# An FFT and MLP-mixer kernel: five PSUM banks for the first chunk, token products ahead of a relu, and a later start of a fold

## The chip, the cores and the metric

The kernel runs on one core of a Trainium2 chip. A core has TensorE (PE: matrix products, which go to PSUM), VectorE (DVE), ScalarE (ACT), GpSimd (POOL) and a sync engine (SP) that issues DMAs; GpSimd and ScalarE issue DMAs too. Each engine works through its own list of instructions in order, and semaphores hold an instruction until what it needs is done. The metric is the device time of one execution in microseconds (us): the median of three runs before was 605.32 us (605.01 to 606.32).

## The reference

The input x is 8 batches of 3008 rows by 256 features. The real part of a Fourier transform over both dimensions goes into a mixer of two layers, one over rows (tokens) and one over features (channels):

```python
X = np.fft.fft(np.fft.fft(x, axis=1), axis=2)
x = X.real                                    # 8 x 3008 x 256
h = np.maximum(x.transpose(0, 2, 1) @ w_tok1, 0.0) @ w_tok2   # 3008 -> 256 -> 3008
u = x + h.transpose(0, 2, 1)
h2 = np.maximum(u @ w_ch1, 0.0) @ w_ch2       # 256 -> 1536 -> 256
out = u + h2
```

## The kernel before

The 3008 rows are taken as 47 x 64, so that the transform over rows is two short transforms, and symmetries of the real part halve the work. For each batch there is a *front*, which makes the u of that batch, and a *main loop*, which makes the channel layer from it.

**The front.** `fold(b, eng)` (L321) adds mirrored parts of the loaded input tiles `xp` and `xm`: four groups of additions (`fa`, `fb`, and three `eo`), then a last step for one row; 17 steps in all. For batches 0 and 1 VectorE does it, for later ones GpSimd. `xm` comes from an indirect gather that GpSimd issues (L109). `front(b)` (L414) then makes `z` (`pz` products, L424), `w` (`pw`, L450 and L452), `rot` (`prot`, L459), the transform `yt` of three chunks (`y(c)`: `py`, L476), the first token layer `uu` (`tok1`: `pt`, L526, with a relu per half `th`), and the second token layer (`tok2(c)`: `pu`, L497), whose sum with `yt` is `ut`, the u of chunk c. A chunk is 512 rows (64 x 8); there are six.

For batch 0 the products `carried()` (`ph`, L403 and L405) must be done as well: they carry w_tok1 through the row transform into `hp` and `hq`, which `tok1` of all batches reads.

**The main loop.** For each chunk there are 12 slots, one for each 128 of the 1536 hidden channels; slot = 12 x chunk + ct. `mm1` (L586) does two products of 128x512 (`pc`, L593, for the halves h of the 256 features) and a relu into the tile `c1`, by ScalarE (`act`, L97) or, for the ct in `on_v`, by VectorE (`ts`, L84). In batch 0 the first three slots are done in one call: the three products for h=0 first, then the three for h=1. The second layer of a chunk is interleaved with the slots of the next: `mm2` (`po`, L698) at every third slot for the first two chunks of batch 0, and later `mm2_seven`, a product of seven multiplications instead of eight (`pa`, `pb`, L643). The first `po` products are at slot 14, and they need all twelve relus of chunk 0. `weight_sums` (L576) makes the weight tiles for `mm2_seven` (`t1w` to `t4w`) on GpSimd, once, at slot 1.

**The order of the work.** It is written out by hand (`manual_schedule`). The functions above are generators, and `take(g, n)` runs n steps of one. L725 to L755 are the prologue, which brings batch 0 to the end of `tok2(0)`. In the loop, `own_at` tells at which slots a step of batch 0's own front is taken: the remaining step of `y(1)`, `tok2(1)`, `y(2)`, and so on, so that the u of chunk 2 is made at slots 20 and 22. Steps of the next batch's front (`nxt`) follow from slot 20 on, the first being `pz`. `fold1`, the fold of batch 1, is taken from slot 9: one step at odd slots, two at even ones. GpSimd's `load_x(2)` at slot 21 fills the `xp` and `xm` that this fold reads.

**PSUM.** There are eight banks, in three kinds: `ps_mm` (tag mm, three, used in turn: `ph`, `pc`), `ps_f` (tag f, three: `pz`, `pw`, `py`, `pt`, `pu`), and `ps_out` (o0 and o1, one each: `po`, `pa`, `pb`). A product that starts in a bank waits until the one that was there has been read.

Of the kernel before, what the change touches and what calls it, by code (L numbers as in the profile page):

```python
# [36 lines left out]
def kernel(  # L37
# [9 lines left out]
    nc = tc.nc  # L47
# [15 lines left out]
    def ps_mm(name):  # L63
        return psum.tile([P, 512], FP32, tag="mm", name=name, bufs=3)

    def ps_out(name, k):
        return psum.tile([P, 512], FP32, tag=f"o{k}", name=name, bufs=1)

    def ps_f(name, dt=FP32, n=512):
        return psum.tile([P, n], dt, tag="f", name=name, bufs=3)  # L70
# [11 lines left out]
    def ts(out_, in_, s1, op0, s2=None, op1=None, eng=V):  # L82
        if op1 is None:
            eng.tensor_scalar(out=out_, in0=in_, scalar1=s1, scalar2=None, op0=op0)  # L84
        else:
            eng.tensor_scalar(out=out_, in0=in_, scalar1=s1, scalar2=s2,  # L86
                              op0=op0, op1=op1)

    def tt(out_, a, b, op, eng=V):
        eng.tensor_tensor(out=out_, in0=a, in1=b, op=op)  # L90
# [4 lines left out]
    def act(out_, in_, scale=1.0, func=AFT.Copy, bias=None):  # L95
        kw = {} if bias is None else {"bias": bias}
        nc.scalar.activation(out=out_, in_=in_, func=func, scale=scale, **kw)  # L97
# [126 lines left out]
    for i in range(2):  # L224
        h = slice(64 * i, 64 * i + 64)
# [51 lines left out]
    for i in range(2):  # L277
        h = slice(64 * i, 64 * i + 64)
# [117 lines left out]
    def carried():  # L396
        for dst, t0, t1 in ((hp, tts[0], tts[1]), (hq, tts[2], tts[3])):
            for g2 in range(NG // 2):
                ph = ps_mm("ph")
                for k in range(2):  # L400
                    g = 2 * g2 + k
                    o = ph[:, k * DTOK:(k + 1) * DTOK]
                    nc.tensor.matmul(o, lhsT=t0[:, g * P:g * P + P], rhs=w1p[:, g, :],  # L403
                                     start=True, stop=False)
                    nc.tensor.matmul(o, lhsT=t1[:, g * P:g * P + P],  # L405
                                     rhs=w1m[:, NG - 1 - g, :],
                                     start=False, stop=True)
                copy(g2 % 2, dst[:, 2 * g2:2 * g2 + 2, :].rearrange("p g k -> p (g k)"),
                     ph[:])
                yield  # L410
# [3 lines left out]
    def front(b):  # L414
# [4 lines left out]
        for t0 in (11, 6, 1):  # L419
            for half in range(2):  # L420
                c = slice(half * P, (half + 1) * P)
                pz = ps_f("pz")
                for k in range(5):
                    nc.tensor.matmul(pz[:, 96 * k:96 * k + 96], lhsT=eo[:, t0 + k, c],  # L424
                                     rhs=t1r, start=True, stop=True)
# [4 lines left out]
        for half in range(2):  # L430
            c = slice(half * P, (half + 1) * P)
            pz = ps_f("pz")
            nc.tensor.matmul(pz[:, 0:24], lhsT=eo[:, 0, c], rhs=t1n[:, half, 0, :],
                             start=True, stop=half == 0)
            if half:
                nc.tensor.matmul(pz[:, 0:24], lhsT=e128[:], rhs=cms[:],
                                 start=False, stop=True)
            nc.tensor.matmul(pz[:, 24:96], lhsT=eo[:, 16, c],
                             rhs=t1b[:].rearrange("p a k -> p (a k)"),
                             start=True, stop=True)  # L440
# [7 lines left out]
        for g in range(NG):  # L448
            pw = ps_f("pw")
            nc.tensor.matmul(pw[:, 0:257], lhsT=zg[:, 1, g], rhs=td1[:],  # L450
                             start=True, stop=False)
            nc.tensor.matmul(pw[:, 0:129], lhsT=zg[:, 0, g], rhs=td0[:],  # L452
                             start=False, stop=True)
# [37 lines left out]
        def tok2(c):  # L491
            w2 = w2v[min(b, 1)]
            nk = 8 if c < 5 else 7
            for h in range(2):
                pu = ps_f("pu")
                for th in range(2):
                    nc.tensor.matmul(pu[:, 0:64 * nk], lhsT=uu[:, th, h, :],  # L497
                                     rhs=w2[:, th, :, 8 * c:8 * c + nk],
                                     start=(th == 0), stop=(th == 1))
                if c < 3:  # L500
                    yv = yt[:, h, 8 * c:8 * c + 8, :]
                else:
                    k0 = NQ - 8 * c
                    yv = yt[:, 1 - h, k0:k0 - nk:-1, ::-1]
                tt(ut[:, c, h, 0:64 * nk].rearrange("p (k b) -> p k b", b=64),
                   pu[:, 0:64 * nk].rearrange("p (b k) -> p k b", b=64), yv, AT.add)
                if h and c < 3:
                    nc.sync.dma_start(out=yt[0:1, :, 8 * c:8 * c + 8, :], in_=yrow[c:c + 1])
                yield

        uu = perb.tile([P, 2, 2, P], FP16, tag="uu", name="uu", bufs=2)
# [59 lines left out]
    def seven(b, c):  # L571
        if c == NCH - 1:
            return b % 2 == 1 and b < BB - 1
        return b > 0 or c >= 2
# [11 lines left out]
    def mm1(b, c, c1, ct, on_v, cts=None):  # L586
        ut = state[b]["ut"]
        n = min(CW, S - CW * c)
        cts = cts or (ct,)
        pcs = [ps_mm("pc") for _ in cts]  # L590
        for h in range(2):
            for pc, ct in zip(pcs, cts):
                nc.tensor.matmul(pc[:, 0:n], lhsT=wc1[:, h, ct * P:(ct + 1) * P],  # L593
                                 rhs=ut[:, c, h, 0:n], start=(h == 0), stop=(h == 1))
        for pc, ct in zip(pcs, cts):
            if ct not in on_v:
                act(c1[:, ct, 0:n], pc[:, 0:n], func=AFT.Relu)
            else:
                ts(c1[:, ct, 0:n], pc[:, 0:n], 0.0, AT.max)
# [120 lines left out]
    def take(g, n):  # L720
        for _ in range(n):
            next(g, None)
# [4 lines left out]
    car = carried()  # L727
# [7 lines left out]
    own = front(0)  # L735
# [13 lines left out]
    for k in range(6):  # L749
        take(own, 2)  # L750
        take(tu_b2, 1 if 0 < k < 4 else 0)
        take(car, 1)
    take(own, 4)
    take(car, 6)
    take(own, 5)  # L755
    setup.close()
    work = ctx.enter_context(tc.tile_pool(name="work", bufs=1))
    w2r = work.tile([P, 2, 64, W2R], FP16, tag="w2r")
# [9 lines left out]
    for b in range(BB):  # L768
        nxt = front(b + 1) if b + 1 < BB else iter(())
        fold1 = fold(1, V) if b == 0 and BB > 1 else iter(())  # L770
        first, done = (20 if b == 0 else 0), 0
        for c in range(NCH):
            fold_at = {42: 5, 54: 5, 66: 7} if b == 0 else {30: 4, 42: 4, 54: 4, 66: 5}
            c1 = work.tile([P, NCT, CW], FP16, tag="c1", name="c1", bufs=2)
            if c == 5 and b % 2:
                G.tensor_copy(out=c1[:, :, 448:512], in_=tail1[:])
            box = {}
            joins = prev is not None and seven(*prev[0:2])
            on_v = ((1, 5, 7, 9, 11), ())[c] if b == 0 and c < 2 else () if joins else (0, 3, 6, 9)
            for ct in range(NCT):  # L780
                slot = NCT * c + ct
                if b == 0 and slot < 3:
                    if slot == 0:
                        mm1(b, c, c1, ct, on_v, range(3))
                else:
                    mm1(b, c, c1, ct, on_v)
                if b == 0 and slot in (4, 16):
                    uT = turn_u(b, c)
                if ct == (11 if b == 0 and c == 1 else 10) and (b, c) not in ((0, 0), (BB - 1, NCH - 1)):
                    uT_next = turn_u(*divmod(NCH * b + c + 1, NCH))  # L790
                if joins:
                    if ct in places:
                        mm2_seven(*prev, places[ct], pbox)
                    if ct in sum_at:
                        sums(prev[2], pbox, sum_at[ct])
                elif prev is not None and ct % 3 == 2:
                    mm2(*prev, ct // 3, pbox)
                if slot == 1 and b == 0:
                    weight_sums()
                if b == 0:  # L800
                    take(own, own_at.get(slot, 0))
                    if 9 <= slot < 21:
                        take(fold1, 2 - slot % 2)
                    if slot == 21 and BB > 2:
                        load_x(2)
                    if slot in (22, 24, 26, 28):
                        th, hb = (slot - 22) // 4, (slot - 22) // 2 % 2
                        G.tensor_copy(out=w2r[:, th, 32 * hb:32 * hb + 32, 0:NQ],
                                      in_=w2v[0][:, th, 32 * hb:32 * hb + 32, :])
                while done < NFRONT * (slot + 1 - first) // (71 - first):  # L810
                    take(nxt, 1)
                    done += 1
                if slot in fold_at:
                    if b + 2 < BB:
                        if slot == min(fold_at):
                            fold2 = fold(b + 2, G)
                        G.tensor_copy(out=hold[:], in_=pbox[4][:, 0, 0, 0:1])  # L817
                        take(fold2, fold_at[slot])
                    if slot == max(fold_at) and b + 3 < BB:
                        load_x(b + 3)  # L820
            if c == 5 and b % 2 == 0:
                G.tensor_copy(out=tail1[:], in_=c1[:, :, 384:448])
            prev, pbox, uT = (b, c, c1, uT), box, uT_next
# [32 lines left out]
```

## Time and profile before

| what | value |
|---|---|
| median of 3 runs | 605.32 us (605.01 to 606.32) |
| the profiled execution | 606.75 us |
| its span, from first to last instruction | 604.9 us |
| TensorE busy | 586.9 us (97%) |
| VectorE, ScalarE, GpSimd busy | 441.4, 386.2, 185.2 us |
| first `pc` product of chunk 0 | 34.54 us |
| gather of batch 1's `xm`, first half: issued, landed | 22.27, 42.56 us |
| first addition of batch 1's fold | 42.68 us |

The profile is one execution. The busy share tells how much of the span an engine had an instruction in work. In the list of slices each digit is the busy share of 1/40 of the span, in tenths. The list of waits names who waited for whom, with total, times and longest. The chain of waits goes back from the last instruction to what released it, step by step, and is printed in order of time as start, length and what it was. In the timeline a row is start, length, engine, line, operation, tiles (written <- read), shapes, count, and in brackets the idle time of the engine before it with what ended it.

### The profile page before, as it was taken

The numbers are of one execution on the slowest core, as the hardware profiler recorded it, in microseconds if no ns is written. First come the engines' busy times: TensorE is split into PE (matmuls) and PEld (weight loads), VectorE is DVE, ScalarE is ACT, GpSimd is POOL, SyncE is SP. The second block draws the span as 40 slices with busy tenths as digits, with TensorE's granted clock in tenths as the row PEclk, the third lists the DMA queues.
The fourth block names the chain that finished last, engine by engine and source line by source line (L and its number), as shares of the span: only waits on it lengthen the run. The fifth ranks groups of instructions, "written<-read, shape, count | busy, mean of one in ns | idle before, by whom it ended". The sixth has DMA issues, their size and how long they took to land.

```text
span 604.9 us, 15073 instructions
## 1 busy us (share of the span) xinstructions
PE 586.9 (97%) x6229; PEld 420.5 (70%) x6229; DVE 441.4 (73%) x886; ACT 386.2 (64%) x749; POOL 185.2 (31%) x260
## 2 busy tenths in 40 slices
PE   4889999999999999999999999999999999999997
PEld 3646676677767776667767777667766777666776
DVE  8778669665988568865888668856688757866663
ACT  8745665486657866477656866568665776546662
POOL 8543144703454044413336033460355000000000
PEclk9999999999999999999999999999999999999999
DMA  8994722573238912492236942366123532233433
GB/s 159 210 175 78 157 50 57 108 124 72 55 71 135 132 36 57 81 186 55 60 80 94 140 88 55 67 135 122 37 54 72 97 60 55 50 88 71 96 70 90
DMA packets 83380, 55.66 MB, mean 92 GB/s; under 512 B 53746, under 2 KB 80050, under 8 KB 82546
## 3 DMA queue, kind: packets, MB, share of 16 engines
q1 hardware_dynamic: 76816, 36.82, 31.7%
q0 software_dynamic: 6176, 17.63, 16.6%
q8 instruction: 48, 0.79, 0.5%
q10 hardware_dynamic: 320, 0.26, 0.2%
q14 instruction: 20, 0.16, 0.1%
HBM read 35.26 MB, written 24.64 MB: 99 GB/s over the span
## 4 chain that ended last, share of the span: by engine, by line
PE 92%; DMA 5%; DVE 1%; POOL 1%; issue 0%; DVEq 0%
PE pc L593 39%; PE pa L643 18%; PE pb L643 14%; PE pu L497 7%; PE po L698 5%; DMA xm<-in_x_dram,ix 3%; PE pt L526 3%; PE py L476 2%; DMA w1m<-in_moe_w_tok_dram 2%; PE pw L450 2%; PE pz L424 1%; PE pw L452 1%; POOL xm L109 0%; DVE ix L86 0%; DVE fb L90 0%
## 5 line engine op out<-in xcount | busy, mean ns | idle before, releaser
L97 ACT ACTIVATE c<-pc 128x512 f16<-128x512 f32 (+1 forms) x551 | 311.0, 590 | 158.4 <-PE pc L593 134.2
L593 PE MATMUL pc<-ut,wc 128*128 128x512 f16 (+1 forms) x1152 | 313.4, 374 | 0.6 <-ACT c L97 0.5
L643 PEld LDWEIGHTS <-s 128*128 128x128 f16 x1968 | 123.4, 98 | 37.8 <-DVE s L90 1.5
L593 PEld LDWEIGHTS <-wc 128*128 128x128 f16 x1152 | 97.9, 98 | 58.1 <-issue 3.7
L643 PEld LDWEIGHTS <-c 128*128 128x128 f16 x1476 | 93.1, 97 | 27.8
L90 DVE TENSOR_TENSOR q<-pa,uT 128x256 f32<-128x256 f32 x123 | 53.1, 432 | 45.3 <-PE pa L643 44.5
L90 DVE TENSOR_TENSOR s<-c 128x1536 f16<-128x1536 f16 x82 | 78.8, 961 | 5.5 <-ACT c L97 5.5
L817 POOL COPY hold<-s 128x1 f16<-128x1 f16 x23 | 4.3, 186 | 254.5 <-DVE s L90 254.5
L90 DVE TENSOR_TENSOR osb<-pb,q 128x256 f32<-128x256 f32 x123 | 52.1, 424 | 33.4 <-PE pb L643 29.7
L90 DVE TENSOR_TENSOR ut<-pu,yt 128x512 f16<-128x512 f32 (+1 forms) x96 | 64.3, 674 | 2.8 <-PE pu L497 2.5
L90 POOL TENSOR_TENSOR eo<-fa,fb 96x512 f16<-96x512 f16 (+1 forms) x48 | 54.2, 1151 | 0.0
L497 PE MATMUL pu<-w2r,uu 128*128 128x512 f16 (+1 forms) x168 | 50.0, 379 | 0.0
L97 ACT ACTIVATE w<-pw 128x257 f16<-128x257 f32 x90 | 34.6, 384 | 10.3 <-PE pw L452 9.0
L90 DVE TENSOR_TENSOR s<-c,s 128x1536 f16<-128x1536 f16 x41 | 38.9, 950 | 0.0
L90 DVE TENSOR_TENSOR s<-s,c 128x1536 f16<-128x1536 f16 x41 | 38.9, 948 | 0.0
L698 PE MATMUL po<-wc,c 128*128 128x256 f16 x288 | 35.6, 273 | 1.6 <-DVE c L84 1.6
L698 PEld LDWEIGHTS <-c 128*128 128x128 f16 x288 | 28.0, 97 | 10.0 <-DVE c L84 1.9
L90 DVE TENSOR_TENSOR osb<-pa,uT 128x256 f32<-128x256 f32 x41 | 17.4, 425 | 23.7 <-PE pa L643 23.7
L643 PE MATMUL pb<-wc,c 128*128 128x128 f16 x492 | 34.4, 219 | 0.0
L643 PE MATMUL pa<-wc,c 128*128 128x128 f16 x492 | 34.4, 219 | 0.0
L643 PE MATMUL pa<-t2w,s 128*128 128x128 f16 x492 | 34.2, 219 | 0.0
L643 PE MATMUL pa<-t4w,c 128*128 128x128 f16 x492 | 34.2, 219 | 0.0
(163 smaller groups left out, 682.4 us busy)
## 6 DMA issues: line engine op xcount, KB each, us to landing
out_dram<-osb SPq DMA_DIRECT2D x83, 256.0 KB
xp<-in_x_dram POOLq DMA_DIRECT2D x14, 408.0 KB, 6.7
out_dram<-osb SPq DMA_DIRECT2D x11, 192.0 KB
uT<-ut SPq DMA_TRANSPOSE x96
w2n<-in_moe_w_tok_dram POOLq DMA_DIRECT2D x2, 752.0 KB, 11.6
w1p<-in_moe_w_tok_dram POOLq DMA_DIRECT2D x2, 384.0 KB, 8.1
wc<-in_moe_w_ch_dram POOLq DMA_DIRECT2D x1, 768.0 KB, 17.7
xp<-in_x_dram POOLq DMA_DIRECT2D x2, 272.0 KB, 6.2
```

Source lines behind the costliest of these rows:

```text
L90: eng.tensor_tensor(out=out_, in0=a, in1=b, op=op)
L97: nc.scalar.activation(out=out_, in_=in_, func=func, scale=scale, **kw)
L424: nc.tensor.matmul(pz[:, 96 * k:96 * k + 96], lhsT=eo[:, t0 + k, c], rhs=t1r, start=True, stop=True)
L450: nc.tensor.matmul(pw[:, 0:257], lhsT=zg[:, 1, g], rhs=td1[:], start=True, stop=False)
L452: nc.tensor.matmul(pw[:, 0:129], lhsT=zg[:, 0, g], rhs=td0[:], start=False, stop=True)
L476: nc.tensor.matmul(py[:, P * k:P * k + P], lhsT=w[:, 4 * c + k, o:o + P], rhs=tab[:, 4 * c + k, :], start=True, stop=True)
L497: nc.tensor.matmul(pu[:, 0:64 * nk], lhsT=uu[:, th, h, :], rhs=w2[:, th, :, 8 * c:8 * c + nk], start=(th == 0), stop=(th == 1))
L526: nc.tensor.matmul(pt[:, o:o + n], lhsT=hw[:, g, c], rhs=w[:, g, w0:w0 + n], start=(g == 0), stop=(g == NG - 1))
L593: nc.tensor.matmul(pc[:, 0:n], lhsT=wc1[:, h, ct * P:(ct + 1) * P], rhs=ut[:, c, h, 0:n], start=(h == 0), stop=(h == 1))
L643: nc.tensor.matmul(dst[:, P * a:P * a + P], lhsT=left[:, k, a, :], rhs=right[:, k, :], start=(first and k + a == 0), stop=(k == NH - 1), s ...
L698: nc.tensor.matmul(po[:, o:o + D], lhsT=c1[:, ct, ks * P:ks * P + P], rhs=wc2[:, ct, 0:D], start=(ct == 0), stop=(ct == NCT - 1))
L817: G.tensor_copy(out=hold[:], in_=pbox[4][:, 0, 0, 0:1])
```

## The change

Three edits, all in batch 0's first chunks:

- In `tok2`, for the first chunk of batch 0, the products of the first half (`th` = 0) for both h are issued into two `ps_mm` banks ahead, as a step of their own; the second halves follow as before. In the prologue, four groups of `carried` are taken one by one between the steps of `rot` and `y(0)`, two more after them; the count of `own` is one more for the added step.
- `mm1` takes the banks o0 and o1 beside the three of tag mm for chunk 0 (ct modulo 5 below 2), and VectorE's relus in that chunk are those of ct 1, 5, 8 instead of 1, 5, 7, 9, 11.
- `fold1` is taken from slot 12 to 23 instead of 9 to 20, one step at even slots, two at odd ones.

```diff
         def tok2(c):
             w2 = w2v[min(b, 1)]
             nk = 8 if c < 5 else 7
+            whole = b == 0 and c == 0
+            if whole:
+                pus = [ps_mm("pu") for _ in range(2)]
+                for h in range(2):
+                    nc.tensor.matmul(pus[h][:], lhsT=uu[:, 0, h, :], rhs=w2[:, 0, :, 0:8],
+                                     start=True, stop=False)
+                yield
             for h in range(2):
-                pu = ps_f("pu")
-                for th in range(2):
+                pu = pus[h] if whole else ps_f("pu")
+                for th in range(1 if whole else 0, 2):
                     nc.tensor.matmul(pu[:, 0:64 * nk], lhsT=uu[:, th, h, :],
...
-        pcs = [ps_mm("pc") for _ in cts]
+        pcs = [ps_out("pc", k % 5) if b + c == 0 and k % 5 < 2 else ps_mm("pc") for k in cts]
...
-    take(own, 4)
-    take(car, 6)
-    take(own, 5)
+    for k in range(4):
+        take(own, 1)
+        take(car, 1)
+    take(car, 2)
+    take(own, 6)
...
-            on_v = ((1, 5, 7, 9, 11), ())[c] if b == 0 and c < 2 else () if joins else (0, 3, 6, 9)
+            on_v = ((1, 5, 8), ())[c] if b == 0 and c < 2 else () if joins else (0, 3, 6, 9)
...
-                    if 9 <= slot < 21:
-                        take(fold1, 2 - slot % 2)
+                    if 12 <= slot < 24:
+                        take(fold1, 1 + slot % 2)
```

## The prediction

> **What bounds the kernel now.** I began with the page's busy shares and slices.
>
> ```profile
> PE 586.9 (97%) x6229; PEld 420.5 (70%) x6229; DVE 441.4 (73%) x886; ACT 386.2 (64%) x749; POOL 185.2 (31%) x260
> ...
> PE   4889999999999999999999999999999999999997
> ```
>
> TensorE is busy except in the first slices (15.1 us each): whatever is worth having lies before about 50 us. Next, what TensorE waited for (total, times, longest), whole run:
>
> ```profile
> PE po L698 <- DVE c L84: 1.6, 1, 1.6
> PE pz L424 <- ACT z L97: 0.6, 1, 0.6
> PE pw L450 <- ACT z L97: 0.6, 1, 0.6
> PE pc L593 <- ACT c L97: 0.5, 2, 0.3
> PE pz L433 <- ACT z L97: 0.5, 2, 0.3
> PE pu L497 <- DVE uv L90: 0.5, 1, 0.5
> PE py L476 <- DVE w L460: 0.3, 1, 0.3
> ```
>
> The largest is one wait of 1.62 us at 46.49; the same view from 46.7 us to the end shows none besides. So a microsecond that TensorE gains by 50 us stays gained, unless it makes a new wait. The chain of waits in order of time shows what made this one:
>
> ```profile
> 22.27 20.29 DMA xm<-in_x_dram,ix
> ...
> 42.68 1.01 DVE fa L90
> 43.69 1.68 DVE fb L90
> 45.37 0.46 DVE eo L90 x2
> 45.83 0.61 DVE c L84
> 46.44 0.04 issue
> 46.49 0.28 PE po L698
> ```
>
> The gather of batch 1's rows lands at 42.56. VectorE has stood at the first addition of batch 1's fold since slot 9; behind it in the same queue is the relu of slot 11 (chunk 0's last), and TensorE's first second-layer product (slot 14) needs that tile. The timeline gives the prices:
>
> ```profile
> 43.37 1.72 POOL L90 TENSOR_TENSOR t4w<-wc,t2w 128x768 f16<-128x768 f16 x1
> 43.62 1.76 DVE L90 TENSOR_TENSOR fb<-xm,xp 96x512 f16<-96x512 f16 x1
> 45.75 0.68 DVE L84 TENSOR_SCALAR c<-pc 128x512 f16<-128x512 f32 x1
> 46.49 0.28 PE L698 MATMUL po<-wc,c 128*128 128x256 f16 x1 [1.62 <-DVE c L84]
> 50.67 1.27 DVE L90 TENSOR_TENSOR yt<-py,sqy 128x512 f16<-128x512 f32 x2
> 52.99 0.68 DVE L90 TENSOR_TENSOR ut<-pu,yt 128x512 f16<-128x512 f32 x1
> 54.22 0.38 PE L424 MATMUL pz<-t1n,eo 96*128 96x96 f16 x5
> ```
>
> fb takes 1.76 us beside GpSimd's t4w, and 0.41 us in the next group: the first fold group can't end much before t4w does (45.09).
>
> **What the Trainium skill says.** "SBUF — State Buffer", SBUF: two separate sides: VectorE with two SBUF inputs and a GpSimd operation that reads SBUF take an exclusive lock, and the later one stands until the first ends. The trace agrees: fb ends 45.37, 0.28 us after t4w. "PSUM — Partial Sum Buffer", Specifications: 8 banks of 512 FP32 values per partition; the kernel has 3+3+2 in three pools, and a 128x512 product fills one. Same page, Engine vs sequencer instructions: the compute queues are strict FIFO and matmuls start in program order, which is how slot 11's relu could hold TensorE.
>
> **The change, part by part.** Prices are steps from start to start in the timeline. The built order of the instructions says what is queued behind what.
>
> *Carried products between the steps of y(0).* One group of four `ph` products now stands before py's first half and one before its second. Before, TensorE idled 0.34 us for the rotated column, 0.22 us and briefly again for banks, and the first `pt` started at 29.29. After: prot 25.11, then `ph` (4 x 0.11), py (0.22), `ph`, py, then four groups (1.76) end near 28.2; three banks allow about that. But two of the evacuations (0.6 us each on VectorE) now stand behind the two yt operations, which start at about 27.3, end near 28.6, so the last `hq` copy ends near 29.8, against 30.18. The second half of tok1 starts near 30.0 instead of 30.64: 0.6 us earlier.
>
> *Token products of the first half ahead.* Two `pu` products (0.26 each) move into the 0.46 us wait for the second half's relu. The first sum `ut` then waits for one product instead of two (0.26 off), and the second no longer for the chain pu, pu (34.62 before). Before, the four took from 33.07 to 34.58. I give it 0.45 us. They use banks of the `mm` pool, which the `ph` products left long ago. Chunk 0's first h=1 products come at 34.3 instead of 35.37: 1.05 us for both parts.
>
> *Five banks and three VectorE relus for chunk 0.* The waits of 0.25 and 0.26 us for a bank (39.63, 40.91) go. ScalarE has 9 relus instead of 7: 9 x 0.5 = 4.5 us against at least 6.1 us of products (24 + 4 of them, 0.216 and 0.26): not the limit. The fifth of the relus, slot 11's, is out of VectorE's queue. From 34.3, TensorE has three products left of slots 0 to 2 (0.65), `pu` 0.52, two slots 0.86, `pu` 0.52, eight slots 3.45, py 0.22, two slots 0.86: 7.1 us, so the first `po` starts near 41.4 and ends (12 x 0.11) near 42.7, where it was at 46.6 before. So up to here it is 3.9 us ahead. Banks o0 and o1 that `po` then takes were emptied by ScalarE at slots 10 and 11, more than 1 us before.
>
> *Fold from slot 12.* The same instructions; the gather is not moved. VectorE still waits for 42.56, so the head start meets a line fixed in time. What comes out at its end: the next thing that TensorE needs of VectorE is a bank of the `f` pool for the second `pz` (slot 22). That bank holds the first `pu` of chunk 2, emptied by the `ut` at 52.99 in the timeline above. In the new order that `ut` has ahead of it three fold groups instead of four, and no relu. Off: 0.60 (relu) + 0.34 + 0.34 + 0.11 + 0.34 + 0.34 (group 4) = 2.07 us, so it starts at 50.9 and ends at 51.6. Everything else ahead of it stays (three groups, osb 0.67, yt 1.19). From the first `po`'s end to this pz TensorE took 7.6 us (46.6 to 54.22), so without waiting it is there near 50.3; it waits 1.3 us and starts at 51.65, against 54.22: 2.55 us ahead. About 1.3 us of the 3.9 are absorbed there.
>
> Next late thing: the third `pz` needs ScalarE's copy of the second (done by 52.6, used at 53.6): no wait. The pz after slot 25 uses in the new order the bank of the pz before it, whose ScalarE copy (0.62 us; one took 0.84) begins when that pz ends near 55.15 and ends near 55.8; TensorE is there at 55.35: 0.45 us lost. Then 2.1 us stay.
>
> *Edits and moves at nothing.* Group 4 and the fold's last step end at about 55.1 instead of 54.06, so GpSimd's issues of batch 2's loads (54.30 before) and the w2r copies behind them come 1 us later: covered, since the first use of w2r is at about 95 us and batch 2's fold starts at slot 42, beyond 80. If that cover were gone it would cost that 1 us. osb of slot 17 runs at about 47.2, 2.4 us earlier; its transposes are issued 38.88 before and a microsecond earlier now, behind y(1)'s row on SP. ScalarE's relus of chunk 1 are as before. There is no operation or byte more.
>
> Sum: 2.55 - 0.45 = 2.1 us. The profiled execution took 606.75 (span 604.9), so it would take 604.65 (span 602.8). Against the median of 605.32 that is **603.2 us**. 0.2% of it, 1.2 us, is about what a measurement of this kernel can tell from no change.
>
> Not shown in the trace of before: where the earlier transposes (about a microsecond sooner, near 40 us) meet the last of the gather on the DMA engines. From below: nothing, even a gain of 0 since the transfer isn't changed. From above: their packets, about 0.9 us of all engines' time if the gather stood behind all of them. But a first addition that starts at 43.4 instead of 42.68 still ends with t4w: then only up to 0.4 us reaches the `ut`. I take 0 and keep 0.4 for the range. The bank switch costs: the trace has five tiles open nowhere; I take no price beyond the waits, and keep 0.3 to either side.
>
> **The rivals.**
> *R1, the fold binds less than I think.* If fa and fb shed their wait for GpSimd, 1.9 us of VectorE's time goes (1.01 + 1.76 against 0.42 + 0.41), the `ut` ends before TensorE comes to its pz, and 3.9 - 0.45 us stay: 601.9. For it: in the new order VectorE has nothing else to do from 39.4 to 42.6, so a gather that lands sooner would be used at once. Against: GpSimd's weight sums are tied to wc's landing at 37.6 and unchanged.
> *R2, only the visible wait goes.* Everything else is absorbed at pz, with copies of 0.84 us and more on the way: 2.1 - 0.4 - 0.2 = 1.5 us and less, 603.8 to 604.2. For it: several banks are freed by VectorE in close sequence from 50 to 56 us.
> *R3, the stall only moves.* If the `ut` or the pz tiles behind the fold are later than worked out by 1.5 us or more (one more fold group ahead of it), what is left is below 0.6 us: 605. Against: the built order has three groups there.
> *R4, slower.* The gather is pushed out by the transposes and the row DMAs that now come earlier. Chunk 2's `ut` moves with it once the first addition starts after 45.09 (t4w's end; the lock no longer hides it). fa and fb then take 0.7 us, so the fold is late by the start + 0.7 - 45.37. It decides against the change where that passes 2.1 us, at a landing near 46.7, and at 49 gives 607.6. Against: these DMAs hold 0.9 us of work.
>
> **How the numbers follow.** Forecast 0.62, R1 0.12, R2 0.13, R3 0.07, R4 0.06. The forecast's own range is 602.5 to 603.8 (0.4 up for the gather, 0.3 either way for banks). For eight in ten the range takes in R1 at its lower end and R2 and the better part of R3 at its upper, and leaves out R4 and the rest of R3 (1 in 10), with the far side of each for the rest: 601.8 to 604.7. Faster by over 0.2% is below 604.1: forecast, R1 and most of R2, 0.85. Within 0.2%: 0.09. Slower by over 0.2%: 0.06.
>
> **What would show it.** In the profile after: `po`'s wait for c at 46.5 gone; first `po` near 41.4; the fold's first addition still at 42.6 behind the gather; a new wait of TensorE, pz for `ut`, of about 1.3 us ending near 51.6; one of about 0.45 for z near 55.8; no others after. Chunk 0's first relu near 34.8 instead of 35.83. The prediction falls if the gather lands at another time, if pz's wait is over 2 us or absent, or if TensorE waits anew after 60 us.

## The result, and the profile after

| | before | after |
|---|---|---|
| median, runs beside each other (six each) | 606.31 us (605.01 to 606.51) | 604.38 us (603.80 to 604.73) |
| ratio | | 0.9973 (95%: 0.9960 to 0.9986) |
| the profiled execution, its span | 606.75, 604.9 us | 603.80, 601.9 us |

The change takes 1.9 us off; 603.2 with a range of 601.8 to 604.7 had been predicted, from a drop of 2.1. The time is right, but of the forecast's list the wait of 1.3 us at `pz` and the first addition at 42.6 can't be found in this profile. Both stand among the forecast's own signs of being wrong (the gather lands at another time; the wait of `pz` is absent): the sum held, the path to it did not. First the page of the changed kernel, busy times and slices:

```profile
PE 586.4 (97%) x6229; PEld 420.1 (70%) x6229; DVE 438.1 (73%) x884; ACT 387.2 (64%) x751; POOL 184.6 (31%) x260
...
PEclk9899999999999999999999999999999999999999
```

TensorE's busy time is the same to 0.5 us. The second slice of the granted clock has an 8; the page of the kernel before has nines throughout. The waits of TensorE in the changed kernel, whole run (total, times, longest):

```profile
...
PE pz L424 <- DVE eo L90: 1.5, 2, 1.2
PE pz L424 <- ACT z L97: 0.6, 2, 0.5
...
PE pc L600 <- DVE ut L90: 0.3, 1, 0.3
...
```

The `po` wait of 1.6 us is gone, as forecast. The 0.5 us for `z` is there, as forecast. The wait of 1.3 us of a `pz` for `ut` is not there. The chain of waits of the changed kernel, in order of time (start, length, what), shows the stretch that was forecast:

```profile
33.89 1.46 PE pc L600 x6
...
41.79 1.33 PE po L705 x12
43.13 0.43 PE pc L600 x2
...
50.74 0.21 PE pz L424 x5
...
53.90 0.23 PE pz L424 x5
54.12 0.02 issue
54.15 0.82 ACT z L97
54.97 0.04 issue
55.01 0.37 PE pz L424 x5
```

From 33.89 to 54.12 every piece of the chain is TensorE's; then it waits for the copy `z`. It walks past the fold, which was to hold it at 51.6. The timeline of the changed kernel says why:

```profile
25.52 0.18 PE L459 MATMUL prot<-w,lrot 128*128 128x12 f16 x1
...
41.73 1.65 DVE L90 TENSOR_TENSOR fa<-xp,xm 96x512 f16<-96x512 f16 x1 [2.02 <-DMA xm<-in_x_dram,ix]
43.31 0.41 DVE L90 TENSOR_TENSOR fb<-xm,xp 96x512 f16<-96x512 f16 x1
49.69 0.68 DVE L90 TENSOR_TENSOR ut<-pu,yt 128x512 f16<-128x512 f32 x1
55.01 0.37 PE L424 MATMUL pz<-t1n,eo 96*128 96x96 f16 x5 [0.47 <-ACT z L97]
```

The gather is in by 41.7 instead of 42.6, GpSimd's `t4w` ends at 43.10 instead of 45.09, and so the first fold group's `fb` ends at 43.72 instead of 45.37. On the other side `prot`, late in the prologue, starts at 25.52 instead of 25.11. Neither is in what the edits touch: this is another execution, not only another kernel. What differs up to `prot` is above all the granted clock. By stretches of 2 us (length; busy time of TensorE, its weight loads, VectorE, ScalarE, GpSimd with instructions; clock; DMA share; GB/s), the profile of the kernel before that the prediction was built on:

```profile
18.00:20.00 2.00, 1.28 (x11) 0.78 (x11) 1.54 (x3) 1.35 (x4) 1.35 (x3) 1.00 1.13 202
20.00:22.00 2.00, 1.93 (x17) 1.49 (x17) 1.06 (x3) 1.71 (x6) 1.97 (x3) 1.00 1.20 233
```

and the changed kernel:

```profile
18.00:20.00 2.00, 1.66 (x9) 1.00 (x9) 1.51 (x3) 0.96 (x3) 1.32 (x2) 0.50 1.14 204
20.00:22.00 2.00, 2.00 (x16) 1.45 (x15) 0.57 (x2) 1.56 (x3) 1.81 (x3) 0.70 1.16 225
```

The clock is at half for 3.4 us, from 17.8 to 21.2 us. Is that the change, or chance? And what do the 1.6 us at `po` and the 1.3 us at `pz` rest on?

### The profile page after: what moved, and what is told of

The parts are those of the page before. It is cut to its first block, busy times and chain, and to the rows that moved or that the text cites. A ratio compares the mean times of both kernels' runs of the same rounds, so it can differ in the third digit from the quotient of the medians.

```text
span 601.9 us, 15073 instructions
## 1 busy us (share of the span) xinstructions
PE 586.4 (97%) x6229; PEld 420.1 (70%) x6229; DVE 438.1 (73%) x884; ACT 387.2 (64%) x751; POOL 184.6 (31%) x260
## 4 chain that ended last, share of the span: by engine, by line
PE 95%; ACT 2%; DVE 2%; DMA 1%; issue 0%; DVEq 0%
PE pc L600 40%; PE pa L650 18%; PE pb L650 14%; PE pu L504 7%; PE po L705 5%; PE pt L533 3%; PE py L476 2%; PE pw L450 2%; PE pz L424 2%; DMA xm<-in_x_dram,ix 1%; PE pw L452 1%; ACT z L97 1%; ACT tts L97 0%; DVE yt L90 0%; DVE eo L90 0%; ACT w L97 0%
## 5 line engine op out<-in xcount | busy, mean ns | idle before, releaser
L650 PEld LDWEIGHTS <-c 128*128 128x128 f16 x1476 | 93.1, 97 | 27.8
L650 PE MATMUL pb<-t1w,s 128*128 128x128 f16 x492 | 34.2, 219 | 0.0
```

What stands on the lines that cost most here:

```text
L650: nc.tensor.matmul(dst[:, P * a:P * a + P], lhsT=left[:, k, a, :], rhs=right[:, k, :], start=(first and k + a == 0), stop=(k == NH - 1), s ...
```

## The experiments

The accounts to be told apart: the forecast's (1.6 us goes at `po`, of a head start of 3.9 us the fold takes 1.3 back, `z` another 0.45); R1 (the fold doesn't bind, the front and the banks bring the gain by themselves); and R2 (only the visible wait goes). "Before" stands for the kernel before run beside the others. Below, a run "with the dip" is one with a mean granted clock of 0.997 or less; the others are at 0.998 to 1.00. In all ten profiles with such a mean the clock stands at 0.50 for 3.41 us, beginning between 17.8 and 20.2 us; in the four others it is full until the last few us of the span. For runs without a profile the mean alone is known, and the runs were sorted by it after they were made. Medians of few runs (2 to 8 in most groups) tell a few tenths of a us at best.

**The kernel before, again** (no edit).

> The kernel before, unchanged, to see how far its own executions spread. Both theories: ratio 1.000, interval holding 1. What is asked of its profile: where wc2 and the gather of batch 1 land (37.6 and 42.6 us before; 35.8 and about 41.7 in the profile after the change, though nothing that is issued earlier was changed), and whether the granted clock dips at 15 to 30 us (0.997 after, 1.0 before). If landings and clock differ here too, the differences belong to the execution, not to the change.

606.13 us, ratio 0.9999 (0.9991 to 1.0008). Its profile is another execution of the same program. From its timeline, `prot`, the first twelve `po`, and the fifth `pz` of the next front:

```profile
26.27 0.18 PE L459 MATMUL prot<-w,lrot 128*128 128x12 f16 x1
...
44.69 1.50 PE L698 MATMUL po<-wc,c 128*128 128x256 f16 x12
...
57.43 0.38 PE L424 MATMUL pz<-t1n,eo 96*128 96x96 f16 x5
```

The twelve `po` stand in one row: there is no wait among them, and yet the profiled span is 604.3, 0.6 us under the one with the 1.6 us wait. This profile has the dip (clock 0.80, 0.50, 0.84 from 18 to 24 us), `prot` starts at 26.27, and `fb` ends at 44.44. So the dip is not made by the change, and the largest wait that the prediction was built on is absent from this execution. Over all 101 runs of the kernel before that stood beside experiments, 57 have the dip (median 606.31) and 44 don't (605.66).

**The front alone.**

```diff
+            whole = b == 0 and c == 0
...
-    take(own, 4)
-    take(car, 6)
-    take(own, 5)
+    for k in range(4):
+        take(own, 1)
+        take(car, 1)
+    take(car, 2)
+    take(own, 6)
```

> The kernel before with the first edit alone (token products of the first half ahead, carried products between the steps of y(0)); relus, banks and fold as before. Theory 1, the head start is absorbed by what VectorE does at the fold: slot 11's relu still stands behind the gather, fa and fb, so TensorE only waits longer at po (1.62 us becomes about 2.6): 0.0 us, within 0.3. Theory 2, the parts add up: 1.0 us faster.

605.41, ratio 0.9994 (0.9986 to 1.0003). With the dip 605.40 (6 runs) against 606.31; without it 605.44 (7 runs) against 605.66: 0.9 us, near Theory 2, in the one group and 0.2, near Theory 1, in the other. In its profile the first h=1 product of chunk 0 comes 9.19 us after `prot`, where it was 10.26 in the profile before: 1.07 us. Part of that meets the `po` wait; its timeline:

```profile
42.71 1.76 DVE L90 TENSOR_TENSOR fb<-xm,xp 96x512 f16<-96x512 f16 x1
43.69 1.38 PE L705 MATMUL po<-wc,c 128*128 128x256 f16 x11
44.85 0.68 DVE L84 TENSOR_SCALAR c<-pc 128x512 f16<-128x512 f32 x1
45.58 0.28 PE L705 MATMUL po<-wc,c 128*128 128x256 f16 x1 [0.51 <-DVE c L84]
```

The twelfth `po` starts 1.11 us after `fb`'s end (44.47), as in the profile before (45.37 to 46.49). So a front that is faster by itself gains what the fold's first group allows.

**Banks and relus alone.**

```diff
-        pcs = [ps_mm("pc") for _ in cts]
+        pcs = [ps_out("pc", k % 5) if b + c == 0 and k % 5 < 2 else ps_mm("pc") for k in cts]
...
-            on_v = ((1, 5, 7, 9, 11), ())[c] if b == 0 and c < 2 else () if joins else (0, 3, 6, 9)
+            on_v = ((1, 5, 8), ())[c] if b == 0 and c < 2 else () if joins else (0, 3, 6, 9)
```

> The kernel before with the second edit alone (five banks, VectorE's relus at ct 1, 5, 8); fold from slot 9. Theory 1: po's wait of 1.62 us and the bank waits (0.5) go, but chunk 2's first ut stands behind four fold groups as before and comes only 0.6 us (one relu) or so earlier; TensorE waits for it at pz: 0.6 to 1.1 us faster, with a new wait pz for ut of about 1 us. Theory 2: 2.1 us faster and no new wait.

605.02, ratio 0.9982 (0.9975 to 0.9988): the largest part of the three. With the dip 605.36 (11 runs, 0.95 under before), without it 604.21 (10 runs, 1.45 under). From the first h=1 product to the first `po` it takes 7.10 us instead of 8.11, and no `po` waits. In its profile, which has the dip, the `pz` of slot 22 waits for the `ut`, as Theory 1 had it, though for less than 1 us:

```profile
43.42 1.76 DVE L90 TENSOR_TENSOR fb<-xm,xp 96x512 f16<-96x512 f16 x1
...
52.15 0.68 DVE L90 TENSOR_TENSOR ut<-pu,yt 128x512 f16<-128x512 f32 x1
...
52.88 0.37 PE L424 MATMUL pz<-t1n,eo 96*128 96x96 f16 x5 [0.23 <-DVE ut L90]
```

From `fb`'s end (45.18) to the `ut`'s end (52.83) are 7.65 us, with four fold groups ahead of the `ut`. The forecast's third edit was meant to take one of them away.

**The fold's place alone.**

```diff
-                    if 9 <= slot < 21:
-                        take(fold1, 2 - slot % 2)
+                    if 12 <= slot < 24:
+                        take(fold1, 1 + slot % 2)
```

> The kernel before with the third edit alone (fold from slot 12); VectorE keeps the relus of ct 1, 5, 7, 9, 11 and there are three banks. Theory 1: slot 11's relu now comes ahead of the fold, so po's wait goes, and ut comes 1.5 to 2 us earlier: 1.3 to 1.9 us faster, nearly all that the whole change gives (1.9), so that the three parts don't add up. Theory 2, additive: 1.6 us minus what the others give, below 1 us.

605.52, ratio 0.9998 (0.9990 to 1.0007). The 1.3 to 1.9 us of Theory 1 did not come. The groups differ in sign: 606.75 with the dip (6 runs, 0.44 over before), 605.38 without it (8 runs, 0.28 under). Its profile has the dip and the wait for `z` of 0.5 us, so this wait doesn't need the other two parts; the change with the fold at 9 (next) doesn't have it. It comes with the fold's place; that the new order of the `f` banks is how, the moved step below supports.

**The change with the fold at its old place.**

```diff
-                    if 12 <= slot < 24:
-                        take(fold1, 1 + slot % 2)
+                    if 9 <= slot < 21:
+                        take(fold1, 2 - slot % 2)
```

> The changed kernel with the third edit undone (fold from slot 9 again). Theory 1, the later start of the fold is what lets the head start of the other two edits through: chunk 2's first ut comes 1.5 us later, TensorE waits at pz for it by 1 us or more, less the z wait of 0.47 that the new order made: 0.5 to 1.3 us slower than the whole change. Theory 2, the fold's place has no effect or costs 0.5 by the z wait: 0.3 to 0.5 us faster than the whole change.

604.32, ratio 0.9979 (0.9970 to 0.9988); the change beside it (see the next run) 604.64, 0.9971 (0.9961 to 0.9981). Pooled over all runs of each: with the dip 604.41 against 604.65 of the change, without it 604.32 against 603.46. So the fold's place is worth 0.9 us in executions without the dip; in those with it, it seems to cost 0.2 us, which six runs from 604.15 to 606.54 don't settle. The profile of this kernel had no dip (`prot` at 25.01), and the products of slot 22 pay:

```profile
42.69 1.76 DVE L90 TENSOR_TENSOR fb<-xm,xp 96x512 f16<-96x512 f16 x1
...
50.42 0.69 PE L504 MATMUL pu<-w2n,uu 128*128 128x512 f16 x2 [0.71 <-DVE yt L90]
...
51.41 0.68 DVE L90 TENSOR_TENSOR ut<-pu,yt 128x512 f16<-128x512 f32 x1
52.15 0.37 PE L424 MATMUL pz<-t1n,eo 96*128 96x96 f16 x5 [1.04 <-DVE ut L90]
```

From `fb`'s end (44.44) to the `ut`'s end (52.09) are 7.65 us, as with banks and relus alone: the fold's four groups, against three with slot 12. The `pu` before this `pz` already waits for VectorE's `yt`, so the `pz` starts 2.08 us late in all, of which its own row shows 1.04.

**The change again, twice** (no edit).

> The changed kernel unchanged, for a second profile and the spread over executions. In the earlier job the executions of a kernel fell into groups by the granted clock: about 1.0, or about 0.996 where TensorE ran at half speed for some 2 us near 20 us, so that the prologue ended 1.2 us later. Theory 1 (what VectorE does behind the gather binds only in executions whose prologue is not late): 1.6 to 2.0 us faster than before as a median; executions at 1.0 about 2.1 us faster than those of before at 1.0 (605.86), with the wait pz for ut in such a profile; those at 0.996 about 1.7 faster (three parts: 1.05 + 1.0 - 0.45), without that wait. Theory 2 (the fold never binds): the same gain in both groups.

> The change once more, for a profile of it. If its profile falls in an execution with the clock at 1.00: prot at 25.0 to 25.1, first chunk-0 product of h=1 at 34.0, first po at 41.1. The prediction then has the pz of slot 22 wait for chunk 2's ut by 1.3 us, to 51.6; the rival, that the gather lands a microsecond earlier than in the profile of the kernel before and the fold ends in time, has no such wait and pz at 50.1. If it falls in one at 0.996 to 0.997, it should repeat the first two profiles of the change: no wait for ut, one of 0.5 for z.

604.64, ratio 0.9971 (0.9961 to 0.9981), and 604.32, 0.9966 (0.9952 to 0.9980). Both profiles fell in executions with the dip (`prot` at 26.84 and 26.26), repeat the first one, no wait for `ut` and 0.5 us for `z`, and leave the question for an execution without the dip open at this point. Over the 19 runs of the change: 604.65 with the dip (12), 603.46 without (7).

**GpSimd's weight sums out of the way.** They start at slot 22 instead of 1, so no GpSimd operation stands beside the fold.

```diff
-                if slot == 1 and b == 0:
+                if slot == 22 and b == 0:
                     weight_sums()
```

> The changed kernel with GpSimd's weight sums at slot 22 instead of slot 1, so that no GpSimd operation runs beside fa and fb of the first fold group. fa plus fb then take 0.8 us instead of 2.1 (2.8 in the profile of before), and chunk 2's ut comes 1.2 us or more earlier. Theory 1: no gain where the prologue is late (ut isn't waited for there), up to 1.3 us at clock 1.0; as a median 0 to 0.6 us. Theory 2, the fold never binds: 0 in both. If t3w and t4w come too late for the second layer of chunk 3, slower, with TensorE waiting for them near 75 us.

603.31, ratio 0.9967 (0.9955 to 0.9978). With the dip 604.82 (3 runs; the change 604.65), without it 603.21 (5 runs; the change 603.46). Its timeline shows the lock gone:

```profile
42.17 0.42 DVE L90 TENSOR_TENSOR fa<-xp,xm 96x512 f16<-96x512 f16 x1 [1.52 <-DMA xm<-in_x_dram,ix]
42.52 0.41 DVE L90 TENSOR_TENSOR fb<-xm,xp 96x512 f16<-96x512 f16 x1
```

`fa` and `fb` take 0.42 and 0.41 us instead of up to 1.76, as "SBUF — State Buffer", SBUF: two separate sides, has it of the Trainium skill, with no GpSimd operation to stand behind. Yet the medians move by no more than 0.25 us either way. The 1.9 us of VectorE that R1 would have gained were not worth 1.9 us of the kernel: the three profiles of the change, all with the dip, have no wait for this `ut`, and the one without the dip, below, has one of 0.3 us.

**The step of batch 0's front at slot 24 moved to slot 25**, against the wait for `z`.

```diff
-    own_at = {1: 1, 2: 1, 4: 1, 12: 1, 15: 1, 18: 1, 20: 1, 22: 1, 24: 1, 27: 1, 30: 1, 33: 1,
+    own_at = {1: 1, 2: 1, 4: 1, 12: 1, 15: 1, 18: 1, 20: 1, 22: 1, 25: 1, 27: 1, 30: 1, 33: 1,
```

> The changed kernel with the step of tok2(4) taken at slot 25 instead of 24. A pu then stands between the pz whose bank the next pz takes and that next pz, so that ScalarE's copy of z (0.6 to 0.8 us) is hidden. If the wait of 0.47 us (pz for z) is what the change still costs, it goes, and the time falls by 0.45 us in every group, whatever the fold does. If VectorE's order is what holds pz there, the wait only changes its name and nothing is gained.

> The same without the dummies, beside them on the same chip. Both theories: two groups as before, about 603.1 where the mean clock is 1.00 and 604.3 where it is 0.996 to 0.997, and 0.3 to 0.4 below the change itself in each group.

(The table `own_at` holds steps of batch 0's own front; one of them moves past the next `pz`, so that the `f` banks are taken in another order. The expectation of the run with dummies, below, calls it a step of `front(1)`, which it is not.) 603.92, ratio 0.9966 (0.9953 to 0.9979), and 604.21, 0.9958 (0.9944 to 0.9972). Over both: 604.29 with the dip (6 runs), 603.00 without (4), that is 0.36 and 0.46 below the change. The fourth and fifth `pz` then stand in the timeline without a wait:

```profile
53.84 0.38 PE L424 MATMUL pz<-t1n,eo 96*128 96x96 f16 x5
54.26 0.83 ACT L97 ACTIVATE z<-pz 128x480 f16<-128x480 f32 x1 [1.55 <-PE pz L424]
...
55.14 0.37 PE L424 MATMUL pz<-t1n,eo 96*128 96x96 f16 x5
```

The fifth starts 28.99 us after `prot`, where the change has 29.49. The 0.5 us of the `z` wait are a real cost of the new order.

**Against the dip: dummy products in TensorE's gaps.** 31 products of 128x128 whose result nobody reads (the kernel's helper `filler`), between 12 and 19 us, into the moved-step version:

```diff
     take(tu_p, 2)
+    filler(8)
     take(own, 2)
...
-    take(own, 4)
+    for n in (8, 4, 3, 0):
+        take(own, 1)
+        filler(n) if n else None
     take(tu_b0, 1)
+    filler(8)
```

> The change, with its slot-24 step of front(1) moved to slot 25, and with 31 products of the dummy kind (filler, 128x128, into a bank that nothing else uses yet) put into the gaps in which TensorE waits for ScalarE's z copies and VectorE's eo between 12 and 19 us: 8 before the first pz, 8, 4 and 3 between the last four pz, 8 before the first pw. Theory C (the half-speed stretch near 20 us, which some executions have and others not, follows from TensorE's idling in the 4 us before it): no execution shows it, the granted clock of the run is 1.00 every time, prot starts at 25.0 to 25.4 each time, and the time is that of the same kernel's undipped executions, 603.1 +- 0.3, without a second group above it. Rival (the stretch has another cause than TensorE's idling, for instance the moment at which the launch falls): half of the executions or more still have a mean clock of 0.996 to 0.997, prot then starts near 26.2, and the median is 603.9 to 604.4. If the dummies hold up the pz and pw behind them, both theories add up to 0.4.

603.49, ratio 0.9957 (0.9940 to 0.9973), beside 604.21 without the dummies. Four runs, at clocks of 0.998 to 1.00, none above 603.70, while three of the five runs without dummies were at 0.997 and 604.2 to 604.5. The theory's 603.1 +- 0.3 was missed by 0.1 more; that the dummies hold up what stands behind them is likely, and not shown. This is the execution without the dip that was wanted (`prot` at 25.06, clock 1.00 in all stretches), and here the `pz` of slot 22 does wait for the `ut`; up to slot 24 this kernel is, but for the dummies, the change. Its timeline:

```profile
42.43 1.76 DVE L90 TENSOR_TENSOR fb<-xm,xp 96x512 f16<-96x512 f16 x1
...
48.94 0.38 PE L424 MATMUL pz<-t1n,eo 96*128 96x96 f16 x5
...
49.68 0.68 DVE L90 TENSOR_TENSOR ut<-pu,yt 128x512 f16<-128x512 f32 x1
...
50.41 0.37 PE L424 MATMUL pz<-t1n,eo 96*128 96x96 f16 x5
```

The second `pz` starts 1.47 us after the first. In the profiles of the change with the dip it is 1.18. So it comes 0.29 us late, behind a `ut` that ends (50.36) 6.17 us after `fb` (44.19).

**The same dummies in the kernel before.**

> The kernel before with the same 31 dummy products in the gaps between 12 and 19 us, and nothing of the change. Theory C (TensorE's idling lets its clock go to half near 20 us): no execution of it has a mean clock of 0.997 or less, while about half of those of the kernel before beside it have; prot starts at 25.0 to 25.4, and the first po (slot 14) at 43.4 to 43.6. The twelfth po is then held by slot 11's relu, which ends about 1.1 us after the first fold group's fb: it starts at fb's end + 1.1, which with an fb that ends at 44.0 to 45.4 is 45.1 to 46.5 where TensorE alone would be there at 44.85, a wait of 0.3 to 1.65 us, back in the profile. So the median falls by 0.3 to 0.8 us only, to 605.3 to 605.8: what the prologue gains is partly lost at this wait. Rival (another cause of the half-speed stretch): half of the executions show 0.996 to 0.997 as before, the median stays at 606.0 to 606.5, and no po waits for c in a profile with prot near 26.2.

605.91, ratio 0.9995 (0.9987 to 1.0004). None of its 13 runs has the dip; of the 17 runs of the kernel before beside it 9 have. By stretches it now has the full clock:

```profile
18.00:20.00 2.00, 1.56 (x18) 1.17 (x17) 1.52 (x3) 1.00 (x3) 1.43 (x2) 1.00 1.14 204
20.00:22.00 2.00, 2.00 (x19) 1.55 (x18) 1.26 (x3) 1.82 (x5) 1.71 (x3) 1.00 1.16 226
```

`prot` starts at 24.90, and the `po` wait is back, with the twelfth `po` 1.11 us after the end of `fb` (44.62), as in the profile before:

```profile
42.86 1.76 DVE L90 TENSOR_TENSOR fb<-xm,xp 96x512 f16<-96x512 f16 x1
45.00 0.68 DVE L84 TENSOR_SCALAR c<-pc 128x512 f16<-128x512 f32 x1
...
45.73 0.28 PE L698 MATMUL po<-wc,c 128*128 128x256 f16 x1 [1.07 <-DVE c L84]
```

The median is 0.1 us above the expected 605.3 to 605.8, and by its interval no gain is shown: the prologue comes 1.3 us sooner, and the wait eats 1.1 of it. So in the kernel before VectorE's stall takes back most of what an early prologue gains.

## Why the prediction was right, and what in it was not

**One number carries both waits.** Call D the time from `prot`'s start to the end of the fold's first `fb`: how late VectorE is against TensorE. With the idle time taken out, the twelfth `po` of the kernel before starts 19.76 us after `prot` (46.49 - 1.62 - 25.11; also 45.73 - 1.07 - 24.90), and the second `pz` of the change 25.06 after it (50.58 - 25.52, and the same to the hundredth in all five others of the change and its variants with the dip). With the steps of 1.11 and 6.22 us from `fb`'s end to the start of the waiting product (`po` waits as idle time, as the timeline prints them; `pz` waits as lateness of the start):

| profile | D | wait by D | wait measured |
|---|---|---|---|
| before, as read | 20.26 | po 1.61 | 1.62 |
| before, again | 18.17 | none | none |
| before with dummies | 19.72 | po 1.07 | 1.07 |
| front alone (po due 1.08 sooner) | 18.08 | po 0.51 | 0.51 |
| banks and relus alone, fold at 9 (7.70 instead of 6.22; `pz` due 26.35 after `prot`) | 19.04 | pz 0.39 | 0.39 |
| change, three profiles | 18.20, 17.72, 17.69 | none | none |
| moved step, two profiles | 18.35, 17.61 | none | none |
| moved step with dummies | 19.13 | pz 0.29 | 0.29 |
| change with fold at 9 (7.70 instead of 6.22) | 19.43 | pz 2.07 | 2.08 |

TensorE idles at `po` in the kernel before from D = 18.65 on, and comes late at `pz` in the change from 18.84. The steps are read off the rows "before, as read", "moved step with dummies" and "change with fold at 9", so these three are no proof; the others are. (For banks and relus alone, the first `pz` starts 25.17 us after `prot` and the second 1.18 us later where nothing waits.) A profile of the change itself without the dip was not taken.

The idle time understates how late `po` is. A `po` row is 0.28 us long, but the next product starts 0.11 us after it, so 0.17 us of the lateness stand under the row of the eleventh product. By its start the twelfth is due 19.6 us after `prot` (in "before, again" the twelfth of the row of 1.50 us at 44.69 starts at 44.69 + 1.50 - 0.28 = 45.91, 19.64 after `prot`), and the kernel before loses time from D = 18.5 on.

**The 1.62 us at `po` that go, and the 1.3 us at `pz` that are absorbed.** Both mechanisms hold, in this place and with these lengths, the one at `pz` in kernels next to the change and not in a profile of the change itself: the forecast's own fold path was 6.23 us from `fb`'s end to the `ut`'s (45.37 to 51.6), measured 6.17, and it had the four groups at 2.07 us more with the relu in, or 1.47 without; measured 7.65 - 6.17 = 1.48. What was wrong is the step "VectorE still waits for 42.56, so the head start meets a line fixed in time". It took D of one profile for a property of the kernel. At that D of 20.26 the change would wait 1.4 us. Its three profiles have less, and the profile read had the largest D of all those taken. Nor is it the gather's landing that fixes the line: in all but two profiles `fa` or `fb` ends 0.28 or 0.29 us after GpSimd's `t4w`, as the forecast noted for its own, and `t4w` ends anywhere from 43.1 to 45.1. (The two are the fold alone, where the fold starts after `t4w`, and the weight sums out of the way.) The sum came out right because the two terms nearly cancel at any D: where the kernel before loses D - 18.5, the change loses D - 18.84. Nothing in the forecast had worked that out, so this part of its success is luck.

The rest of the sum doesn't depend on D. The fifth `pz` starts 31.16 us after `prot` in "before, again", which has no `po` wait (57.43 - 26.27), and 29.49 in the change (55.01 - 25.52): 1.67 us. Measured between the runs with the dip: 606.31 - 604.65 = 1.66. Where both kernels wait, 0.3 us more, so 2.0, is an estimate from the two thresholds; measured between the runs without the dip: 605.66 - 603.46 = 2.2. The 1.9 of the result lies between.

**The front, 1.05 us.** `prot` to the first h=1 product: 10.26 before, 9.01 in the change, 9.19 with the front alone. The second half of `tok1` starts 4.84 after `prot` instead of 5.53 (0.69; 0.6 was worked out). Of the rest, 0.18 comes from the banks and 0.38 is left for the token products ahead, which had been given 0.45. On the banks: with three, the third product waits for one that the `pu` ahead now hold (with the front alone its products start at 34.76, 34.98 and then 35.36). "They use banks of the `mm` pool, which the `ph` products left long ago" looked at who had the bank before, not at who needs it next.

**Five banks and three VectorE relus.** First h=1 to first `po` in 7.1 us: 7.10 measured, against 8.11. The first `po` is 16.11 after `prot`, 16.3 forecast. Slot 11's relu, out of VectorE's queue, holds nothing in any profile of the change.

**The wait for z, 0.45 us.** 0.47 in all three profiles of the change; the moved step takes it away, and the fifth `pz` then starts 0.51 us sooner. Right in cause, place and size.

**Edits at nothing.** No wait of TensorE after 60 us, as forecast. Not in the list: `pc` for `ut` at 33.89, 0.32 us, since the first sum `ut` now ends after the `pu` that TensorE does meanwhile.

**The base.** The forecast's level rests on the median of three runs, 605.32. Beside the change the kernel before took 606.31, and 101 further runs of it have 606.16. Of the 1.2 us between 603.2 and 604.38, 1.0 is this base, and 0.2 the drop (2.1 against 1.9).

**The rivals.** R1's 601.9 did not come: taking the lock away leaves the time where it was. Its claim that the fold binds less than thought is right in the profiles with the dip. R2's size, 1.5 us and less, is near the 1.7 of the runs with the dip, but for another reason: in the profile of the kernel before with the dip there is no wait at `po` to go, and with the dip the front and the banks bring 0.9 us each by themselves. R3's cause, one more fold group ahead, is the fold at slot 9: 0.9 us in runs without the dip. R4 is out: the gather is in by 41.7 to 42.2 in all profiles of the change, no later than before.

**What beats the change.** The moved step (604.07 over ten runs, against 604.43 of the change over 19), and with the dummies 603.49, ratio 0.9957 (0.9940 to 0.9973). Between these two the four runs with dummies don't decide.

## What to carry to other kernels

A wait in a start-up phase is the difference between two paths of one execution, here a prologue on TensorE, and transfers with GpSimd and VectorE behind them; before it is priced, take a second profile of the same kernel and see whether it is still there. Work out from which lateness on each version waits: if both do from nearly the same one, the wait drops out of the comparison, and the work taken off the path decides. What a part brings alone is not what it brings in company (without the dip, the fold's place brought 0.3 us alone and 0.9 beside the other two), so parts are tried alone and left out. Here only the fold's place was left out; the front and the banks were tried alone.

## What was not expected

TensorE's granted clock falls to 0.50 for 3.41 us near 20 us in all ten profiles with a mean of 0.997 or less, and 57 of 101 executions of the kernel before have such a mean. `prot` then starts at 25.5 to 26.8 instead of 24.9 to 25.1. Idle TensorE stands before it (busy for 1.08 and 1.30 of 2 us from 16 to 18 in "before, again" and the first profile of the change). With 31 dummy products there, none of 17 runs has it, against 12 of 22 beside them without. So the dummies prevent it; but idle time alone doesn't make it, since the profile that the prediction was built on was busy for only 1.06 us in the same stretch and kept the full clock. The Trainium skill ("TensorE: Matmul & The Clock Gate", Part 1: The HAM clock gate) says that an idle window of about 3.4 us halves the clock, and that the window runs freely, so that the same kernel differs from run to run. The trace agrees with both in kind, the 0.50 and the chance of it, and the 3.41 us are as long as that window. But the longest wait between 12 and 19 us in these profiles is 1.2 us, so no whole window was idle: how little work is enough was not tried. Nor is it settled why `fb` ends between 43.7 and 45.4 us in different executions with the weight sums at slot 1. The weight sums start between 35.8 and 37.6 us, with the landing of their weights, and `t4w` ends 7.3 to 7.5 us after; what sets that landing was not tried.
